# Two decode layers on one core: eight cache tiles of one position kept on chip between the two passes

## The chip, the cores and the metric

The kernel runs on one core of one Trainium2 chip. The metric is the device time of one execution in microseconds (us); less is better. Engines are named as in the profile: PE (TensorE matmul), PEld (its weight loads), DVE (VectorE), ACT (ScalarE), POOL (GpSimd), SP (SyncE, which here only issues transfers).

## The reference

Two rows of 448 numbers (a batch of two, one token each) go through attention, a gated feed-forward layer (FFN), the same attention again and the same FFN again. The two attention layers read the **same** key and value caches and weights:

```python
B, Sq, D = 2, 1, 448;  H, Sk, Dh = 16, 4096, 256;  F = 1792      # all float32
def _A_ref(x, k_cache, v_cache, wq, wo):        # caches: [2, 16, 4096, 256]
    q = (x @ wq).reshape(B, Sq, H, Dh).transpose(0, 2, 1, 3)
    p = softmax(einsum("bhqd,bhkd->bhqk", q, k_cache) * Dh ** -0.5)
    return einsum("bhqk,bhkd->bhqd", p, v_cache).transpose(...).reshape(B, Sq, H * Dh) @ wo
def _B_ref(x, W_gate, W_up, W_down):
    gate = x @ W_gate
    return (gate * (gate > 0) * (x @ W_up)) @ W_down
x = A_x
for _ in range(2):
    x = x + _A_ref(layernorm(x), A_k_cache, A_v_cache, A_wq, A_wo)
    x = x + _B_ref(layernorm(x), B_W_gate, B_W_up, B_W_down)
```

Each (head, batch) pair has 4096 keys and 4096 values of 256 numbers, 4 MiB each, so that one pass over both caches reads 256 MiB.

## The kernel before

**Units.** The work of a pass is cut into 32 units, one per (head, batch). A unit's keys lie as 32 tiles of 128 partitions x 256 numbers (128 KiB a tile, 1 KiB per partition), its values likewise. The first pass (`first`) goes through the units in order; the second (`second`) takes the last four first, in reverse order, and then units 0 to 27, so that tiles left over from the end of the first pass are used at once (`keep`, `KEPT`). Position 12 of the first pass is therefore position 16 of the second.

**The arena.** All cache tiles and weights land in one SBUF tile, `arena`: three blocks of eight slots (`BLOCKS`, `PAIR`), each slot eight cache tiles wide (`UNIT`, 1 MiB), and three single slots for weights (`SINGLES`). In the middle of each pass one transfer fills a whole block: four slots of the values of the unit before and four slots of the keys of this unit, 128 rows of 16384 numbers, 8 MiB. A list of loads (`pending`) is written in program order; `pump` issues its head on SP's queue as soon as enough slots are free, and `release`, called when a slot has been read for the last time, runs `pump`. SP waits for the releasing instruction, and later loads wait behind it. A block is free only when its four key slots and its four value slots are.

**One unit, at position u.** `score_block` multiplies all 32 key tiles in place by the query (`tensor_mul`, one DVE instruction over 8192 numbers a partition, L378) and sums each tile (`reduce_sum`, L386). `softmax_max` and `softmax_exp` take the maximum over all keys through POOL (L429) and the exponential on ACT (L434, L437); POOL also adds the sums up (L443). `weigh` then multiplies the probabilities of unit u-1 with its values on PE: 16 matmuls, which the trace shows as 32, into one of two PSUM banks (`po`, L462). `out_copy` on ACT (L475), `out_add` on DVE (L478), `out_turn` on PE (L488) and `project` (L511) bring the result into the output. Order within a turn of the loop is the order of the code: score u, `out_add` and `out_turn` of u-2, softmax of u, then `weigh` and `out_copy` of u-1. Each engine works through its own list in that order.

**Between the passes** `ffn` runs the FFN: `proj` (L576) makes gate and up, `ph` and `ph_tail` turn the hidden row, `block` (L669) multiplies with the third weight, and beside that the query of the second pass's first unit is put together (`ask`, L722 to L748). For the layer norm in it a row of column sums of the query weights is needed: `cols` in PSUM, copied by ACT, scaled, to `turn_cols`, which lies in the last 256 numbers of a weight slot (L637).

**PSUM** has eight banks: one for `pq`, two for `po`, two for `small`, one for `acc`, and two for `pf`, which the queries of each pass's first units and the FFN use in turn.

Of the kernel before, what the change touches and what calls it, by code (L numbers as in the profile page):

```python
# [26 lines left out]
KEPT = 20  # L27
ALONE = 25

SUMS = 96  # L30
# [40 lines left out]
def two_layers(  # L71
# [17 lines left out]
    ps_a = ctx.enter_context(tc.tile_pool(name="ps_a", bufs=1, space=PSUM))  # L89
    ps_f = ctx.enter_context(tc.tile_pool(name="ps_f", bufs=2, space=PSUM))  # L90
# [9 lines left out]
    blocks = set()  # L100

    def source(key, n):
# [12 lines left out]
    def pump():  # L115
        while pending:
            (kind, name, c), n = pending[0]
            last = at_of.get((kind, name, c - 1)) if kind in "kv" else None
            at = units.take(n, kind, last)
            if at is None:  # L120
                return
            pending.pop(0)
            src = source((kind, name, c), n)
            dst = arena[:, at * UNIT : at * UNIT + src.shape[1]]
            parts = [0, src.shape[1]]
            if not pending:
                parts[1:1] = [src.shape[1] - CLOSE * TAIL]
            elif len(pending) == 1:
                parts[1:1] = [8 * P]
            for i, j in zip(parts, parts[1:]):  # L130
                nc.sync.dma_start(dst[:, i:j], src[:, i:j])
            for k in range(n):
                key = (kind, name, c + k)
                if n == PAIR:
                    key = ("k", name, k - NC) if k >= NC else ("v", behind[name], k)
                at_of[key] = at + k
            if n >= NC:
                blocks.add((kind, name))

    def get(*key):  # L140
        at = at_of[key]
        return arena[:, at * UNIT : (at + 1) * UNIT]

# [88 lines left out]

    po_all = ps_o.tile([P, 2, 2 * DH], F32, name="po")
    nc.vector.memset(po_all, 0.0)

# [59 lines left out]
    def attention(order, after, q_first=None, begun=None):  # L295
# [60 lines left out]
        def first_query():  # L356


            if q_first is None:
                total = squares()  # L360
                query_of(0, ps_f.tile([P, B, DH], F32, name="pf"))
            else:
                q_of[0] = q_first
                total = begun()
            deviation(total)
            query_of(1, ps_f.tile([P, B, DH], F32, name="pf"))
            unread = work.tile([P, 1], F32, name="sums")
            nc.scalar.activation(unread, eps_t, AF.Exp)

        def score_block(u, c):  # L370


            at = at_of["k", order[u], 0] * UNIT
            kt = arena[:, at : at + NC * UNIT].rearrange("p (t n) -> p t n", t=NT)
            if c == 0:
                s_of[u] = work.tile([P, NT], F32, name="scores")
            if c == 0:
                nc.vector.tensor_mul(kt, kt, q_of[u][:, None, :].to_broadcast([P, NT, DH]))  # L378
            shared = 0 if (WHOLE_SECOND if ahead else WHOLE_FIRST)[0] <= u < ALONE else CT
            if c == 0:  # L380
                for t in range(shared):
                    nc.scalar.activation(  # L382
                        kt[:, t, :], kt[:, t, :], AF.Copy, accum_out=s_of[u][:, t : t + 1]
                    )
            if c == NC - 1:
                nc.vector.reduce_sum(s_of[u][:, shared:], kt[:, shared:, :], axis=AX.X)  # L386
# [65 lines left out]
        def weigh(u, c):  # L452
# [5 lines left out]
            if c == 0:  # L458
                po_of[u] = po_all[:, u % 2]
            for t in range(CT // 2):  # L460
# [99 lines left out]
    def ffn(last):  # L560
# [8 lines left out]

        def proj(parts):  # L570

            p = ps_f.tile([P, D], F32, name="pf")
            for n, (part, c, done) in enumerate(parts):
# [40 lines left out]

        pg = proj([(0, 0, True), (1, 1, True), (2, 2, True), (3, 3, False)])
        add_rows(SUMS, lead, stop=last)
# [6 lines left out]
        inverse()  # L623
        scaled = work.tile([P, B], F32, name="scaled")
        nc.vector.tensor_mul(scaled, sel, rstd)
        nc.vector.tensor_mul(scaled, scaled, rstd)
        if not last:
            nscaled = work.tile([P, B], F32, name="nscaled")
# [5 lines left out]
        pu = proj([(3, 4, True), (4, 0, True), (5, 1, True), (6, 2, True)])  # L634
        if not last:
            turn_cols = w_q[:, FULL * DH + P + 2 * D :]
            nc.scalar.activation(turn_cols, cols, AF.Copy, scale=nscaled[:, b : b + 1])  # L637
        nc.vector.tensor_mul(hid, pu, hid)
# [3 lines left out]

        ph = ps_f.tile([P, FULL, P], F32, name="pf")
        ph_tail = ps_q.tile([P, P], F32, name="pq")
        for m in range(FULL):
# [29 lines left out]
        if last:  # L675


            square = work.tile([P, B], F32, name="square")
# [6 lines left out]
            y_end = ps_f.tile([P, TAIL], F32, name="pf")[SUMS : SUMS + B]  # L685
            nc.tensor.matmul(y_end, unit, y_end_row, start=True, stop=False)
            pds = [po_all[:, 0, :D], ps_f.tile([P, D], F32, name="pf")] * 2

# [26 lines left out]

        q = ps_f.tile([P, DH], F32, name="pf")

# [11 lines left out]

        pd = po_all[:, 0, :D]  # L730
        sums = work.tile([P, FULL + 1], F32, name="sums4")
        total = work.tile([P, 1], F32, name="sums")
        for c in range(FULL + 1):
# [3 lines left out]
            if c > 0:  # L737
                ask(c - 1)
            if c == FULL:
                nc.vector.reduce_sum(total, sums, axis=AX.X)  # L740
            pt = ps_s.tile([P, B], F32, name="small")
# [93 lines left out]
```

## Time and profile before

| | |
|---|---|
| median of 3 runs | 1320.66 us (1320.5 to 1320.78) |
| the profiled execution: its own time / its span from first to last instruction | 1320.27 us / 1318.5 us |
| read from HBM | 562.56 MB |
| busy: PE / DVE / ACT / POOL | 553.7 / 1081.6 / 195.6 / 269.0 us |
| share of the span in which the 16 transfer engines are busy with SP's queue | 99.5% |

In the rows quoted below, a row of the timeline or the chain begins with its start and its length in us; `x2` is a count; what stands in brackets is the idle time of that engine just before, and what ended it. A row of a group of instructions ends in total busy time and the mean in ns of one. `arena<-in_vk_dram` is a load of cache tiles.

### The profile page before, as it was taken

The numbers are of one execution on the slowest core, as the hardware profiler recorded it, in microseconds if no ns is written. First come the engines' busy times: TensorE is split into PE (matmuls) and PEld (weight loads), VectorE is DVE, ScalarE is ACT, GpSimd is POOL, SyncE is SP. The second block draws the span as 40 slices with busy tenths as digits, with TensorE's granted clock in tenths as the row PEclk, the third lists the DMA queues.
The fourth block names the chain that finished last, engine by engine and source line by source line (L and its number), as shares of the span: only waits on it lengthen the run. The fifth ranks groups of instructions, "written<-read, shape, count | busy, mean of one in ns | idle before, by whom it ended". The sixth has DMA issues, their size and how long they took to land.

```text
span 1318.5 us, 9085 instructions
## 1 busy us (share of the span) xinstructions
PE 553.7 (42%) x3276; PEld 190.6 (14%) x3276; DVE 1081.6 (82%) x780; ACT 195.6 (15%) x776; POOL 269.0 (20%) x192
## 2 busy tenths in 40 slices
PE   2243342433434324345585444242433424434348
PEld 2011010110111101112141111110111101101113
DVE  4989888898888988888729987798888988877892
ACT  2100000000000000212026513000000000012241
POOL 0002003322133220321001153030123331230210
PEclk9675666656667667666697777666767667666679
DMA  9999999999999999999999999999999999999998
GB/s 408 435 430 429 432 428 437 432 436 434 417 445 435 430 430 426 445 418 430 421 405 416 431 430 435 438 432 430 432 431 436 433 428 436 429 432 425 427 425 334
DMA packets 22665, 563.16 MB, mean 427 GB/s; under 512 B 2520, under 2 KB 2652, under 8 KB 9564
## 3 DMA queue, kind: packets, MB, share of 16 engines
q1 hardware_dynamic: 22612, 562.57, 99.5%
q8 instruction: 26, 0.43, 0.1%
q14 instruction: 19, 0.16, 0.0%
q10 hardware_dynamic: 8, 0.00, 0.0%
HBM read 562.56 MB, written 0.00 MB: 427 GB/s over the span
## 4 chain that ended last, share of the span: by engine, by line
DMA 55%; DVE 32%; PE 7%; POOL 2%; issue 2%; ACT 1%; DVEq 0%; SPq 0%; POOLq 0%; ACTq 0%
DMA arena<-in_vk_dram 54%; DVE arena L378 12%; DVE scores L386 11%; DVE arena L409 3%; DVE down L418 2%; PE po L462 2%; POOL top L429 2%; DVE arena L418 2%; DMA arena<-in_w_out_dram 1%; DVE row L478 1%; PE small L488 1%; PE acc L511 1%; DVE scores L415 1%; ACT arena L411 1%; PE pf L576 1%
## 5 line engine op out<-in xcount | busy, mean ns | idle before, releaser
L378 DVE TENSOR_TENSOR arena<-arena 128x8192 f32<-128x8192 f32 x51 | 443.3, 8692 | 111.0 <-DMA arena<-in_vk_dram 110.9
L386 DVE TENSOR_REDUCE scores<-arena 128x32 f32<-128x8192 f32 (+1 forms) x53 | 431.8, 8148 | 0.0
L488 PE MATMUL small<-ones,row 128*128 128x1 f32 x256 | 62.0, 346 | 686.3 <-DVE row L478 686.3
L462 PE MATMUL po<-arena,probs 128*2 128x512 f32 x2048 | 303.1, 734 | 10.3 <-DMA arena<-in_vk_dram 6.6
L429 POOL PARTITION_ALL_REDUCE top<-mx x64 | 64.6, 1009 | 645.8 <-DVE mx L427 645.8
L443 POOL PARTITION_ALL_REDUCE total<-rs x64 | 176.1, 2752 | 61.3 <-ACT probs L437 60.3
L488 PEld LDWEIGHTS small<-ones,row 128*128 128x128 f32 x256 | 56.5, 308 | 748.9 <-DVE row L478 748.9
L434 ACT ACTIVATE nm<-top,nsr 128x1 f32<-128x1 f32 x64 | 18.8, 294 | 612.4 <-POOL top L429 612.4
L354 POOL PARTITION_BROADCAST arena<-arena x58 | 27.6, 545 | 300.6 <-ACT arena L350 300.6
L462 PEld LDWEIGHTS po<-arena,probs 128*2 128x2 f32 x2048 | 54.8, 96 | 198.3 <-issue 191.2
L338 PE MATMUL pq<-arena,xs 128*33 128x256 f32 x174 | 70.6, 571 | 14.1 <-DMA arena<-in_w_head_dram 14.1
L511 PE MATMUL acc<-arena,oT 128*2 128x448 f32 x128 | 50.9, 894 | 32.1 <-DVE oT L501 32.1
L350 ACT ACTIVATE arena<-pq 33x256 f32<-33x256 f32 x29 | 10.9, 377 | 321.7 <-PE pq L342 321.7
L382 ACT ACTIVATE arena<-arena 128x256 f32<-128x256 f32 x104 | 41.7, 402 | 86.2 <-DVE arena L378 86.2
L478 DVE SCALAR_TENSOR_TENSOR row<-po,lead,row 128x256 f32<-128x256 f32 x64 | 30.7, 479 | 25.8 <-ACT row L475 25.4
L411 ACT ACTIVATE arena<-arena 128x256 f32<-128x256 f32 x117 | 47.1, 404 | 20.4 <-DVE arena L409 20.1
L409 DVE TENSOR_TENSOR arena<-arena 128x1024 f32<-128x1024 f32 (+1 forms) x24 | 42.0, 1748 | 0.0
L338 PEld LDWEIGHTS pq<-arena,xs 128*33 128x33 f32 x174 | 25.3, 162 | 81.3 <-issue 66.7
L475 ACT ACTIVATE row<-po,lead 128x256 f32<-128x256 f32 x64 | 29.1, 455 | 21.2 <-PE po L462 21.2
L418 DVE SCALAR_TENSOR_TENSOR down<-arena,pq 128x256 f32<-128x256 f32 x64 | 26.9, 420 | 5.4 <-DMA arena<-in_vk_dram 3.4
L501 DVE TENSOR_TENSOR oT<-small,ri 128x4 f32<-128x4 f32 x32 | 5.1, 161 | 29.0 <-PE small L488 29.0
L437 ACT ACTIVATE probs<-scores,nm,sr 128x32 f32<-128x32 f32 x64 | 26.4, 413 | 2.1
(145 smaller groups left out, 359.0 us busy)
## 6 DMA issues: line engine op xcount, KB each, us to landing
arena<-in_vk_dram SPq DMA_DIRECT2D x16, 4096.0 KB, 40.0
arena<-in_w_head_dram SPq DMA_DIRECT2D x31, 896.0 KB, 30.9
arena<-in_vk_dram SPq DMA_DIRECT2D x27, 1024.0 KB, 14.9
arena<-in_vk_dram SPq DMA_DIRECT2D x12, 2048.0 KB, 38.5
arena<-in_w_in_dram SPq DMA_DIRECT2D x14, 896.0 KB, 26.2
arena<-in_w_out_dram SPq DMA_DIRECT2D x5, 896.0 KB, 8.9
arena<-in_vk_dram SPq DMA_DIRECT2D x47, 43.4
arena<-in_w_out_dram SPq DMA_DIRECT2D x1, 512.0 KB, 17.3
```

Source lines behind the costliest of these rows:

```text
L338: nc.tensor.matmul(q, xs[:, c, :], w[:, c * DH : (c + 1) * DH], start=(c == 0), stop=False)
L378: nc.vector.tensor_mul(kt, kt, q_of[u][:, None, :].to_broadcast([P, NT, DH]))
L386: nc.vector.reduce_sum(s_of[u][:, shared:], kt[:, shared:, :], axis=AX.X)
L409: nc.vector.tensor_mul(some, some, q_of[u][:, None, :].to_broadcast([P, whole, DH]))
L411: nc.scalar.activation(kt[:, t, :], kt[:, t, :], AF.Copy, accum_out=found[:, t : t + 1])
L418: nc.vector.scalar_tensor_tensor(junk if kept else kt[:, t, :], kt[:, t, :], 1.0, q_of[u], op0=ALU.mult, op1=ALU.mult, accum_out=found[:, ...
L429: nc.gpsimd.partition_all_reduce(mx_of[u], mx, P, RED.max)
L443: nc.gpsimd.partition_all_reduce(total[:, b : b + 1], rs, P, RED.add)
L462: nc.tensor.matmul(po_of[u][32 * t : 32 * t + 2, :], p_of[u][:, n : n + 2], vt[:, 2 * t * DH : (2 * t + 2) * DH], start=(c == 0), stop=(c ...
L478: nc.vector.scalar_tensor_tensor(row[:, :DH], po_of.pop(u)[:, DH:], lead[:, 1:2], row[:, :DH], op0=ALU.mult, op1=ALU.add,)
L488: nc.tensor.matmul(pT_of[u - u % 2][:, c, b : b + 1], row[:, c * P : (c + 1) * P], ones, start=True, stop=True,)
L511: nc.tensor.matmul(acc[at : at + B], oT_of[h][:, c, :], wo[:, c * D : (c + 1) * D], start=(n < 3), stop=(n >= n_u - 3),)
```

## The change

Eight tiles that the first pass loads at position 12 stay on the chip and are not read again in the second pass.

- **Keys.** The last four key tiles of the unit at position 12 are copied by ACT, before they are overwritten, into two PSUM banks (`spare`, two tiles each). In the second pass DVE multiplies and sums them there: three multiplications and three sums in place of one each. In the first pass the multiplication is split in two, since its second part must wait for the copies.
- **Values.** The first four value tiles of the unit at position 11, which come with the same block, are copied by ACT into 1024 numbers per partition at the end of `arena` (`extra`). PE reads these four tiles from the copy, in both passes.
- **Traffic.** The block's transfer in the second pass is 128 rows of 14336 numbers, not 16384: 1 MiB less. All else is loaded as before, in the same order and into the same slots.
- **Room.** The single slots are 1792 instead of 2048 numbers wide (all that the weights fill), several small tiles share buffers (`scaled` is now named `nm`, `nscaled` `top`, `square` `mx`, `sums4` `rs`), and 768 bytes fewer are set aside for descriptors of transfers issued by POOL, of which there are none. What used `pf` uses the two `po` banks in turn, now two tiles, or in the last FFN the two `spare` banks.
- **Column sums.** `cols` stays in its bank (`pq`) until the FFN's end, where DVE scales it into `row`; ACT's copy is gone. `ph_tail` goes to a `small` bank, since `pq` is taken.

```diff
+SPARED = 12
+KEYS = 4
+VALUES = 4
...
-    arena = consts.tile([P, (BLOCKS * PAIR + SINGLES) * UNIT], F32, name="arena")
+    ps_f = ctx.enter_context(tc.tile_pool(name="ps_f", bufs=1, space=PSUM))
+    arena = consts.tile([P, BLOCKS * PAIR * UNIT + SINGLES * F + VALUES * DH], F32, name="arena")
+    extra = arena[:, -VALUES * DH :]
...
     def source(key, n):
+            if name in spared and n == PAIR:
+                return vk[at, :, VALUES * DH : PAIR * UNIT - KEYS * DH]
...
     def pump():
-            dst = arena[:, at * UNIT : at * UNIT + src.shape[1]]
+            start = place(at) + VALUES * DH * (name in spared and n == PAIR)
+            dst = arena[:, start : start + src.shape[1]]
...
+    po = [ps_o.tile([P, 2 * DH], F32, name=f"po{i}") for i in range(2)]
+    spare = [ps_f.tile([P, 2 * DH], F32, name=f"spare{i}") for i in range(2)]
...
         def score_block(u, c):
+            there = [(kt, 0)]
+            if order[u] == first[SPARED]:
+                most = NT - KEYS
+                held = [bank.rearrange("p (t n) -> p t n", t=2) for bank in spare]
+                there = [(kt[:, :most], 0)]
+                there += [(part, most + 2 * i) for i, part in enumerate(held)]
+                if not ahead:
+                    if c == 0:
+                        for part, t in there[1:]:
+                            nc.scalar.activation(part, kt[:, t : t + 2, :], AF.Copy)
+                        spared.add(order[u])
+                    there[1:] = [(kt[:, most:], most)]
             if c == 0:
-                nc.vector.tensor_mul(kt, kt, q_of[u][:, None, :].to_broadcast([P, NT, DH]))
+                for part, t in there:
+                    n = part.shape[1]
+                    nc.vector.tensor_mul(
+                        part, part, q_of[u][:, None, :].to_broadcast([P, n, DH])
+                    )
...
             if c == NC - 1:
-                nc.vector.reduce_sum(s_of[u][:, shared:], kt[:, shared:, :], axis=AX.X)
+                if shared or not ahead:
+                    there = [(kt[:, shared:, :], shared)]
+                for part, t in there:
+                    found = s_of[u][:, t : t + part.shape[1]]
+                    nc.vector.reduce_sum(found, part, axis=AX.X)
...
         def weigh(u, c):
+            held = c == 0 and order[u] == first[SPARED - 1]
+            if held and not ahead:
+                nc.scalar.activation(extra, vt[:, : VALUES * DH], AF.Copy)
             for t in range(CT // 2):
...
-                    vt[:, 2 * t * DH : (2 * t + 2) * DH],
+                    (extra if held and 2 * t < VALUES else vt)[:, 2 * t * DH : (2 * t + 2) * DH],
...
     def ffn(last):
+        banks = spare if last else po
...
-            turn_cols = w_q[:, FULL * DH + P + 2 * D :]
-            nc.scalar.activation(turn_cols, cols, AF.Copy, scale=nscaled[:, b : b + 1])
...
-        ph_tail = ps_q.tile([P, P], F32, name="pq")
+        ph = banks[0][:, : FULL * P].rearrange("p (m r) -> p m r", m=FULL)
+        ph_tail = ps_s.tile([P, P], F32, name="small")
...
-        pd = po_all[:, 0, :D]
+        pd = po[1][:, :D]
         for c in range(FULL + 1):
             at = block(pd, c, range(14))
...
             if c == FULL:
+                turn_cols = row[:, :DH]
+                nc.vector.tensor_scalar_mul(turn_cols, cols, nscaled[:, b : b + 1])
                 nc.vector.reduce_sum(total, sums, axis=AX.X)
```

Where instructions move: in the fences below, the names after `L` are lines of the one kernel and of the other; `po_108` and `po_109` are the two `po` banks, `spare_112` and `spare_113` the two new ones.

ACT's list around position 12 of the first pass, before: the exponential of one unit is followed directly by `out_copy` (L475) of the unit before it.

```order
L434 ACTIVATE nm<-top,nsr 128x1
L437 ACTIVATE probs,rs<-scores,nm,sr 128x32
L475 ACTIVATE row<-po,lead 128x256
L350 ACTIVATE arena<-pq 33x256
L434 ACTIVATE nm<-top,nsr 128x1
```

The same place after, from the copies of the keys (L400) on:

```order
L400 ACTIVATE spare_112<-arena 128x512
L400 ACTIVATE spare_113<-arena 128x512
L468 ACTIVATE nm<-top,nsr 128x1
L471 ACTIVATE probs,rs<-scores,nm,sr 128x32
L496 ACTIVATE arena<-arena 128x1024
L512 ACTIVATE row<-po_109,lead 128x256
```

The copy of the value tiles (L496) stands behind the exponential of unit 12, and PE's `weigh` of unit 11 reads what it writes.

DVE's list at the end of the FFN between the passes, from the product of gate and up on, before:

```order
L638 TENSOR_TENSOR row<-pf,row 128x448
L652 COPY row<-pf 128x384
L747 TENSOR_TENSOR xs<-xs,small 128x32 x3
L740 TENSOR_REDUCE sums<-sums_1780 128x1
L747 TENSOR_TENSOR xs<-xs,small 64x32 x2
```

and after:

```order
L674 TENSOR_TENSOR row<-po_109,row 128x448
L688 COPY row<-po_108 128x384
L785 TENSOR_TENSOR xs<-xs,small 128x32 x3
L777 TENSOR_SCALAR row<-pq,top 128x256
L778 TENSOR_REDUCE sums<-rs 128x1
L785 TENSOR_TENSOR xs<-xs,small 64x32 x2
```

The scaling of the column sums (L777) now stands on DVE ahead of the sum (L778) that PE's last part of the query waits for; it writes over part of `row`, which PE's `block` matmuls read.

DVE's list at the spared unit in the second pass (position 16), after; before, it was one multiplication and one sum like its neighbours:

```order
L406 TENSOR_TENSOR arena<-arena 128x7168
L406 TENSOR_TENSOR spare_112<-spare_112,arena 128x512
L406 TENSOR_TENSOR spare_113<-spare_113,arena 128x512
L515 SCALAR_TENSOR_TENSOR row<-po_108,lead,row 128x256
L484 RECIPROCAL ri<-total 128x2
L420 TENSOR_REDUCE scores<-arena 128x28
L420 TENSOR_REDUCE scores<-spare_112 128x2
L420 TENSOR_REDUCE scores<-spare_113 128x2
```

Four instructions have come in, two on each side of the row that `out_add` makes.

More of the change, by code (lines that the diff above doesn't have):

```diff
@@ L100, in two_layers @@
     blocks = set()
+    spared = set()
     def source(key, n):
@@ L138, in pump, with place @@
                 blocks.add((kind, name))
+    def place(at):
+        packed = max(0, at - BLOCKS * PAIR)
+        return at * UNIT - packed * (UNIT - F)
     def get(*key):
         at = at_of[key]
-        return arena[:, at * UNIT : (at + 1) * UNIT]
+        return arena[:, place(at) : place(at + 1)]
     def release(*key):
@@ L231, in two_layers @@
     rstd = consts.tile([P, B], F32, name="rstd")
-    po_all = ps_o.tile([P, 2, 2 * DH], F32, name="po")
-    nc.vector.memset(po_all, 0.0)
+    po = [ps_o.tile([P, 2 * DH], F32, name=f"po{i}") for i in range(2)]
+    for bank in po:
+        nc.vector.memset(bank, 0.0)
+    spare = [ps_f.tile([P, 2 * DH], F32, name=f"spare{i}") for i in range(2)]
     acc = ps_a.tile([P, D], F32, name="acc")
@@ L568, in ffn, with proj @@
             w_q = get("h", h, 0)
-        def proj(parts):
-            p = ps_f.tile([P, D], F32, name="pf")
+        banks = spare if last else po
+        def proj(p, parts):
+            p = p[:, :D]
             for n, (part, c, done) in enumerate(parts):
@@ L611, in between @@
                     )
-        pg = proj([(0, 0, True), (1, 1, True), (2, 2, True), (3, 3, False)])
+        pg = proj(banks[0], [(0, 0, True), (1, 1, True), (2, 2, True), (3, 3, False)])
         add_rows(SUMS, lead, stop=last)
@@ L623, in ffn @@
         inverse()
-        scaled = work.tile([P, B], F32, name="scaled")
+        scaled = work.tile([P, B], F32, name="nm")
         nc.vector.tensor_mul(scaled, sel, rstd)
@@ L627, in ffn @@
         if not last:
-            nscaled = work.tile([P, B], F32, name="nscaled")
+            nscaled = work.tile([P, B], F32, name="top")
             nc.vector.tensor_scalar_mul(nscaled, scaled, -1.0 / D)
@@ L633, in ffn @@
             cols = ps_q.tile([P, DH], F32, name="pq")
-        pu = proj([(3, 4, True), (4, 0, True), (5, 1, True), (6, 2, True)])
-        if not last:
-            turn_cols = w_q[:, FULL * DH + P + 2 * D :]
-            nc.scalar.activation(turn_cols, cols, AF.Copy, scale=nscaled[:, b : b + 1])
+        pu = proj(banks[1], [(3, 4, True), (4, 0, True), (5, 1, True), (6, 2, True)])
         nc.vector.tensor_mul(hid, pu, hid)
@@ L712, in ffn @@
             return
-        q = ps_f.tile([P, DH], F32, name="pf")
+        q = po[0][:, :DH]
         def ask(c):
@@ L728, in ask @@
                 )
-        pd = po_all[:, 0, :D]
-        sums = work.tile([P, FULL + 1], F32, name="sums4")
+        pd = po[1][:, :D]
+        sums = work.tile([P, FULL + 1], F32, name="rs")
         total = work.tile([P, 1], F32, name="sums")
@@ L828 @@
     from concourse.bass_utils import run_bass_kernel_spmd as _run
-    nc = _bacc.Bacc("TRN2", target_bir_lowering=False, num_devices=1, dynamic_dma_scratch_size=1024)
+    nc = _bacc.Bacc("TRN2", target_bir_lowering=False, num_devices=1, dynamic_dma_scratch_size=256)
     arrays = _arrays(_np, **inputs)
```

14 lines of the change are left out of this document (6 added, 8 removed).

## The prediction

> **What bounds the kernel now.** I read the page's slices first, to see whether any engine or the transfers are busy throughout.
>
> ```profile
> DVE  4989888898888988888729987798888988877892
> DMA  9999999999999999999999999999999999999998
> q1 hardware_dynamic: 22612, 562.57, 99.5%
> arena<-in_vk_dram SPq DMA_DIRECT2D x47, 43.4
> ```
>
> DVE, the busiest engine, has gaps in most slices. The transfers have none before the last slice. The last row is the 47 whole-block loads: 43.4 us from issue to landing. Next the stages, cut at the FFN between the passes and at the end; the last two columns are the share of time in which the transfer engines are busy and their GB/s.
>
> ```profile
> 2.00:660.00 658.00, 260.54 (x1399) 87.97 (x1403) 557.36 (x367) 63.01 (x228) 130.35 (x93) 0.66 1.00 431
> 668.00:672.00 4.00, 3.90 (x37) 1.23 (x36) 0.94 (x6) 0.02 (x1) 0.00 (x0) 1.00 0.79 297
> 672.00:1300.00 628.00, 266.57 (x1599) 91.80 (x1597) 517.33 (x381) 127.32 (x536) 138.27 (x94) 0.69 1.00 430
> 860.00:1160.00 300.00, 112.77 (x638) 36.37 (x638) 263.11 (x76) 20.02 (x67) 69.57 (x44) 0.67 1.00 432
> 1300.00:1310.00 10.00, 9.78 (x79) 3.31 (x77) 2.75 (x12) 0.70 (x2) 0.00 (x0) 1.00 1.01 414
> 1310.00:1318.50 8.50, 5.42 (x128) 3.63 (x126) 1.84 (x8) 1.49 (x6) 0.00 (x0) 1.00 0.26 99
> ```
>
> The transfers run full from 2 to 668 us and from 672 to 1310 us. The one hole, 668 to 672 us, is 0.21 x 4 = 0.84 us of idle; after 1310 us only the last weights and the tail are left. So time is bytes over rate, and the next question is how far ahead of DVE the queue runs. These are DVE's multiplications at positions 15 to 17 of the second pass (the spared unit is 16), and SP's longest wait:
>
> ```profile
> 954.02 8.69 DVE L378 TENSOR_TENSOR arena<-arena 128x8192 f32<-128x8192 f32 x1 [1.31 <-DMA arena<-in_vk_dram]
> 975.64 8.69 DVE L378 TENSOR_TENSOR arena<-arena 128x8192 f32<-128x8192 f32 x1 [2.45 <-DMA arena<-in_vk_dram]
> 994.93 8.69 DVE L378 TENSOR_TENSOR arena<-arena 128x8192 f32<-128x8192 f32 x1 [1.33 <-DMA arena<-in_vk_dram]
> SPq L131 <- DVE scores L386: 697.4, 52, 34.4
> ```
>
> DVE waits for data at each unit, 1.3 to 2.45 us. SP waits for DVE to free a block, but that does not hurt: of the 43.4 us of a block load, its own 8.39 MB at 432 GB/s are 19.4 us, so 24.0 us pass between the issue and its first bytes, nearly all of it other loads. That is the cover of every step below in this stretch.
>
> **Part 1, the bytes.** Eight tiles are 8 x 131072 = 1.049 MB fewer. In the stage that holds position 16 (860 to 1160 us) the rate is 432 GB/s: 2.43 us less. Nearest rows for other rates: 414 GB/s (narrow weight rows, 1300 to 1310 us) gives 2.53 us, so 2.4 to 2.55 us. I take 2.43, because the shortened rows stay long. By the Trainium skill's "HBM Reference", section "Specifications (TRN2)", a core's share of HBM is about 358 GB/s, by which the same bytes would be worth an estimated 2.93 us; the trace disagrees, with 432 GB/s on this core alone.
>
> **Does the gain reach the end?** The chain of waits, in order of time:
>
> ```profile
> 1177.20 43.65 DMA arena<-in_vk_dram
> 1220.97 8.69 DVE arena L378
> ...
> 1300.25 14.69 DMA arena<-in_w_out_dram
> ```
>
> The last block starts DVE at 1220.97 us, and from there to 1300.25 us the chain holds no transfer: DVE and then PE set the releases of the last loads. A block that lands 2.43 us sooner starts that stretch 2.43 us sooner, since DVE is idle ahead of each of the units between, and the last loads are still queued (14.69 us from issue to landing of one piece). So all of it moves together.
>
> **Part 2, position 12 of the first pass.** What stands there now; the multiplications are those of units 12 and 13:
>
> ```profile
> 262.60 8.69 DVE L378 TENSOR_TENSOR arena<-arena 128x8192 f32<-128x8192 f32 x1 [2.48 <-DMA arena<-in_vk_dram]
> 272.68 6.52 PE L462 MATMUL po<-arena,probs 128*2 128x512 f32 x32
> 280.41 0.33 SPq L131 DMA_DIRECT2D arena<-in_vk_dram  x1
> 280.65 0.35 POOL L429 PARTITION_ALL_REDUCE top<-mx  x1 [18.67 <-DVE mx L427]
> 281.68 0.19 ACT L437 ACTIVATION_READ_ACCUMULATOR probs<-scores,nm,sr 128x1 f32 x1
> 281.91 8.69 DVE L378 TENSOR_TENSOR arena<-arena 128x8192 f32<-128x8192 f32 x1 [1.36 <-DMA arena<-in_vk_dram]
> 281.95 8.89 POOL L443 PARTITION_ALL_REDUCE total<-rs  x1 [0.96 <-ACT probs L437]
> 290.52 0.48 DVE L478 SCALAR_TENSOR_TENSOR row<-po,lead,row 128x256 f32<-128x256 f32 x1
> 294.08 0.33 SPq L131 DMA_DIRECT2D arena<-in_w_head_dram  x1
> L475 ACT ACTIVATE row<-po,lead 128x256 f32<-128x256 f32 x64 | 29.1, 455 | 21.2 <-PE po L462 21.2
> L382 ACT ACTIVATE arena<-arena 128x256 f32<-128x256 f32 x104 | 41.7, 402 | 86.2 <-DVE arena L378 86.2
> L263 ACT ACTIVATE row<-row 2x448 f32<-2x448 f32 x1 | 0.6, 575 | 0.0
> ```
>
> ACT takes 402 ns for 256 numbers and 575 for 448, 0.9 ns each: about 0.63 us for 512 and 1.09 us for 1024. No row shows ACT writing PSUM; between 0.4 us (the 256-wide row) and twice 0.63, I take 0.63, as the row nearest in width is 575. The two key copies end near 263.9 us, long before DVE has done its first 28 tiles (7.6 of the 8.69 us, to 270.2). They cost DVE one instruction more, some 0.1 us, inside its 1.36 us of idle.
>
> The value copy costs more in order than in time. It stands behind unit 12's exponential, which ends at 281.87, so ends near 283.0. `weigh` of unit 11, now at 272.68, waits for it: 6.52 us of matmuls, done at 289.5. Three things stand behind. `out_copy` on ACT then ends near 290.0 (0.45 us), and DVE wants it at 290.52: just in time, and if not, DVE's idle of some 2 us a unit takes it. `out_turn` on PE follows DVE as before. And the load that SP issued at 280.41 goes out near 289.5, as its block now holds unit 11's values until then: 9.1 us later, out of 24.0 us of cover. SP's next load, a head's weights, was issued 13.67 us after, so nothing queues up behind. Cost nothing; without that cover, 9.1 us.
>
> **Part 3, position 16 of the second pass.** The sum that unit 16 has now, and DVE's nearest row with a wide PSUM input:
>
> ```profile
> 984.72 8.66 DVE L386 TENSOR_REDUCE scores<-arena 128x32 f32<-128x8192 f32 x1
> L638 DVE TENSOR_TENSOR row<-pf,row 128x448 f32<-128x448 f32 x2 | 1.2, 624 | 7.9 <-PE pf L576 7.9
> ```
>
> 624 ns for 448 against 8.69 us for 8192 (1.06 ns each): 512 numbers take 0.55 us by the long row and 0.71 by the short one. Two multiplications and two sums of 512 instead of 1024 more in each long one: 4 x 0.71 - 2 x 1.09 = 0.7 us more; if writing PSUM doubled the multiplications, 2.1 us. No row shows that write; I take 0.7, as the row nearest in size says. DVE's 2.45 us of idle ahead of unit 16 let it start with its data, 2.43 us sooner; unit 17's data come sooner by as much, and the 1.33 us of idle ahead of that unit hold the 0.7. At 2.1 DVE would be 0.8 us late there, gone by the next unit's idle, and SP's releases with it, under the 24.0 us. Cost nothing. PE reads four value tiles at another address, which costs nothing either.
>
> **Part 4, the FFN between the passes**, where the queue is thinnest. The end of the query's chain, and the six 1 MiB loads issued from 690 to 705 us:
>
> ```profile
> 686.02 0.64 PE L669 MATMUL po<-arena,row 128*32 128x64 f32 x28
> 686.13 0.19 DVE L747 TENSOR_TENSOR xs<-xs,small 128x32 f32<-128x32 f32 x1 [1.66 <-PE small L744]
> 687.05 0.16 DVE L740 TENSOR_REDUCE sums<-sums 128x1 f32<-128x4 f32 x1 [0.74 <-ACT down L736]
> 687.43 0.70 PE L748 MATMUL pf<-arena,sums 128*128 128x256 f32 x2
> 688.62 0.42 DVE L418 SCALAR_TENSOR_TENSOR arena<-arena,pf 128x256 f32<-128x256 f32 x1 [0.66 <-PE pf L725]
> arena<-in_vk_dram SPq DMA_DIRECT2D x6, 1024.0 KB, 8.3
> SPq L131 <- PE pf L576: 5.9, 3, 5.2
> ```
>
> The scaling of `cols` on DVE writes over `row`, so it waits for the last `block` matmul (686.66) and takes about 0.45 us (256 numbers from PSUM; L478 above takes 0.48), to 687.15; the sum then ends at 687.3 instead of 687.21, ahead of L748 at 687.43. Cost 0 to 0.45 us on this chain. A load here lands 8.3 us after issue, 2.5 us of it its own bytes, so 5.8 us, less its start-up, lie ahead of it: 0.45 us is covered. The hole at 668 to 672 us comes earlier: SP waits for the first PE matmuls of `proj` (the last row, from 664 to 672 us), which no edit delays. It stays. The new PSUM banks add only waits for reads long done; I cost the renamed buffers at nothing too.
>
> **The sum.** 1320.27 (this execution; 1318.5 of it the span) - 2.43 = 1317.84. The median of the runs lies 0.39 above this execution, so 1320.66 - 2.43 = **1318.2 us**. 0.2%, about what a measurement of this kernel can tell from no change, is 2.64 us: below 1318.02 counts as faster. The forecast is 0.184%, just inside.
>
> **The rivals.**
> - *More than the bytes* (0.24): the bytes are worth 2.55 us and the hole of 0.84 us in part closes, as the releases there shift. Against it: no edit is ahead of the hole. Up to 2.55 + 0.84 = 3.39 us: 1317.3. By 0.25 us above forecast it counts as faster. The skill's 358 GB/s would land here too, at 1320.66 - 2.93 = 1317.7 us; I give that 0.02 of the 0.24.
> - *Part of the gain is lost* (0.10): the thin queue after the FFN runs dry for a while, or the stretch from 1220.97 us turns out bound by DVE and PE alone, and then the last loads come no sooner. For it: no transfer in that part of the chain. Against: it starts with one. 1318.5 to 1320.7.
> - *Slower, by the late release at position 12* (0.06): the block load that leaves at 280.41 now hangs on ACT, behind POOL's maximum. It decides at 24.0 us of delay, when the queue runs dry; 9.1 is the sum above. If PE's `weigh` also had to sit out POOL's 8.89 us row and one more unit (20.45 us, half the 40.91 us between the multiplications of positions 15 and 17), 38.4 us late, 14.4 us dry: 1320.66 - 2.43 + 14.4 = 1332.7. With one unit alone, 29.6 us late and 5.6 dry: 1323.8. For it: the one new wait that a load hangs on. Against: the maximum takes 0.35 us there.
> - That the change does not do what it says is ruled out by the load itself, 14336 numbers wide instead of 16384.
>
> **How the numbers follow.** Forecast 0.60, rivals 0.24, 0.10, 0.06. The forecast's own spread (0.14 us of the runs, 2.4 to 2.55 us of the bytes, 0.45 us of Part 4) is 1317.9 to 1318.7, with a small part below 1318.02. Faster: 0.24 and 0.04 of the forecast, 0.28. Same: 0.56 and 0.10, 0.66. Slower: 0.06. The range, leaving out the slow rival and the ends of the two others: 1317.4 to 1319.3.
>
> **What would show it.** Right: HBM read 1.05 MB less; transfers still 0.99 to 1.01 busy in all stages but 668 to 672 us, where the hole stays near 0.84 us; `weigh` of unit 11 near 283 us, and a block load issued near 289.5 that still lands before DVE wants it, three units after 262.60; unit 17 of the second pass starting about 2.4 us sooner than 994.93. Wrong: a stage with a share below 0.97 after 283 us or after 690 us, a DVE wait above 3 us at positions 13 to 16 of the first pass, or a tail after the last load other than now.

## The result, and the profile after

| | before | after |
|---|---|---|
| median, same chip | 1320.81 us (1320.5 to 1321.43, 15 runs) | 1318.33 us (1317.98 to 1318.87, 15 runs) |
| the profiled execution / its span | 1320.27 / 1318.5 us | 1318.33 / 1316.6 us |
| read from HBM | 562.56 MB | 561.52 MB |

After over before is 0.9982 (95% interval 0.9975 to 0.9988): 2.48 us less, against a forecast of 2.43.

The page of the kernel after: slices of DVE and of the transfers, the loads' queue, HBM, and two of the issues (size where it is even, and us from issue to landing). The row with 7168.0 KB is the block load that has become narrower.

```profile
DVE  4989888898888988788829987698898988877892
DMA  9999999999999999999999999999999999999998
q1 hardware_dynamic: 22612, 561.53, 99.5%
...
HBM read 561.52 MB, written 0.00 MB: 427 GB/s over the span
...
arena<-in_vk_dram SPq DMA_DIRECT2D x1, 7168.0 KB, 41.0
...
arena<-in_vk_dram SPq DMA_DIRECT2D x46, 43.2
```

The stages of the kernel after, cut as in the prediction (the last three columns: PE's granted clock, the transfers' busy share, GB/s):

```profile
2.00:660.00 658.00, 256.65 (x1393) 88.89 (x1394) 557.59 (x369) 65.27 (x231) 137.81 (x93) 0.68 1.00 431
668.00:672.00 4.00, 3.91 (x43) 1.95 (x44) 1.55 (x10) 0.74 (x1) 0.00 (x0) 1.00 0.69 244
672.00:1300.00 628.00, 273.86 (x1623) 92.98 (x1622) 519.16 (x391) 126.89 (x535) 146.25 (x94) 0.68 1.00 429
860.00:1160.00 300.00, 114.85 (x638) 36.82 (x638) 265.82 (x80) 20.05 (x67) 78.28 (x44) 0.66 1.00 433
```

The picture is that of before: transfers full in both passes at the same rate, and one hole at 668 to 672 us. The hole is larger here, 0.31 x 4 = 1.24 us against 0.84; the experiments come back to that.

### The profile page after: what moved, and what is told of

It reads as the page before. It is cut to its first block, busy times and chain, and to the rows that moved or that the text cites. A ratio compares the mean times of both kernels' runs of the same rounds, so it can differ in the third digit from the quotient of the medians.

```text
span 1316.6 us, 9091 instructions
## 1 busy us (share of the span) xinstructions
PE 555.1 (42%) x3276; PEld 192.1 (15%) x3276; DVE 1082.8 (82%) x787; ACT 197.4 (15%) x778; POOL 284.4 (22%) x192
## 3 DMA queue, kind: packets, MB, share of 16 engines
HBM read 561.52 MB, written 0.00 MB: 427 GB/s over the span
## 4 chain that ended last, share of the span: by engine, by line
DMA 56%; DVE 30%; PE 7%; POOL 3%; issue 2%; ACT 1%; SPq 0%; DVEq 0%; POOLq 0%; ACTq 0%
DMA arena<-in_vk_dram 53%; DVE scores L420 11%; DVE arena L406 11%; POOL top L463 3%; DVE down L452 2%; PE po L499 2%; DMA arena<-in_w_in_dram 2%; DVE arena L443 2%; DVE arena L452 2%; DMA arena<-in_w_out_dram 1%; DVE row L515 1%; PE small L525 1%; PE acc L548 1%; PE pq L352 1%; ACT arena L445 1%
## 5 line engine op out<-in xcount | busy, mean ns | idle before, releaser
L406 DVE TENSOR_TENSOR arena<-arena 128x8192 f32<-128x8192 f32 (+2 forms) x52 | 442.3, 8507 | 105.3 <-DMA arena<-in_vk_dram 104.6
L420 DVE TENSOR_REDUCE scores<-arena 128x32 f32<-128x8192 f32 (+2 forms) x53 | 430.8, 8128 | 0.0
L463 POOL PARTITION_ALL_REDUCE top<-mx x64 | 80.4, 1256 | 626.0 <-DVE mx L461 626.0
L352 PE MATMUL pq<-arena,xs 128*33 128x256 f32 x174 | 74.7, 597 | 13.1 <-DMA arena<-in_w_head_dram 13.1
L445 ACT ACTIVATE arena<-arena 128x256 f32<-128x256 f32 x117 | 47.1, 404 | 20.4 <-DVE arena L443 20.1
## 6 DMA issues: line engine op xcount, KB each, us to landing
arena<-in_vk_dram SPq DMA_DIRECT2D x1, 7168.0 KB, 41.0
```

The source lines that it names most:

```text
L352: nc.tensor.matmul(q, xs[:, c, :], w[:, c * DH : (c + 1) * DH], start=(c == 0), stop=False)
L406: nc.vector.tensor_mul(part, part, q_of[u][:, None, :].to_broadcast([P, n, DH]))
L420: nc.vector.reduce_sum(found, part, axis=AX.X)
L445: nc.scalar.activation(kt[:, t, :], kt[:, t, :], AF.Copy, accum_out=found[:, t : t + 1])
L463: nc.gpsimd.partition_all_reduce(mx_of[u], mx, P, RED.max)
```

## The experiments

Two theories stood at the start. **Bytes**: the kernel is bound by its transfers, the gain is the 1 MiB not read, and all edits around it are covered by the queue. **Sum of edits**: the 2.48 us are a larger gain, less what the copies, the late release or the FFN edits cost. The rival to the cover itself is that a late release costs more, or less, than its delay beyond the queue.

### All edits but the bytes, and the bytes alone

`e1_all_but_bytes` is the kernel after, loading the whole block again in pass 2, so that the spared tiles are read and not used:

```diff
-            if name in spared and n == PAIR:
-                return vk[at, :, VALUES * DH : PAIR * UNIT - KEYS * DH]
...
-            start = place(at) + VALUES * DH * (name in spared and n == PAIR)
+            start = place(at)
```

> The changed kernel in all its edits (copies, split multiplications, PSUM operands, column sums in PSUM, renamed buffers), but the block at position 16 of the second pass is loaded whole again, 16384 numbers a row. Theory 'bytes over rate': the other edits cost and earn nothing, so the time of the kernel before comes back, 1320.8 us within 0.3 us (ratio 0.9998 to 1.0002). Rival 'the other edits earn part of it' (one ACT copy less between the passes, other PSUM banks): 1318.4 to 1320.3 us. Rival 'the other edits cost, and the bytes earn more than 2.43 us' (by a core's share of 358 GB/s 2.93 us): 1321.2 us or more.

Measured: 1320.36 us (1319.88 to 1320.82, 11 runs) beside 1320.85 of the kernel before; ratio 0.9997 [0.9989, 1.0006]. That is 0.14 us below the expected range and not as low as either rival put it; `e6_no_tiles_spared` comes back to it.

`e2_bytes_alone` is the kernel before with the narrower load in pass 2 and nothing else; the eight tiles there are computed from what an earlier load left in the slots.

```diff
...
+            if name == first[12] and n == PAIR and name in seen:
+                return vk[at, :, 4 * DH : PAIR * UNIT - 4 * DH]
...
-            dst = arena[:, at * UNIT : at * UNIT + src.shape[1]]
+            start = at * UNIT + 4 * DH * (name == first[12] and n == PAIR and name in seen)
+            dst = arena[:, start : start + src.shape[1]]
+            if n == PAIR:
+                seen.add(name)
```

> The kernel before with one edit: the block at position 16 of the second pass is loaded 14336 numbers wide, and nothing is copied, so that eight tiles of that position are computed from old contents of the arena. Theory 'bytes over rate': 2.43 us less than before, 1318.4 us within 0.3 us (ratio 0.9980 to 0.9983). Rival 'the other edits earn part': less than 2.0 us gained here. Rival 'other edits cost': more than 2.8 us gained here.

Measured: 1318.24 us (1317.8 to 1319.1, 11 runs); ratio 0.9981 [0.9972, 0.999]. The bytes alone give what the whole change gives, and all the rest together gives nothing that can be told from no change.

### Four times the bytes

`e3_bytes_x4` is `e2_bytes_alone` with 16 tiles in place of 4 left out at each end of the block: 4 MiB less.

```diff
-                return vk[at, :, 4 * DH : PAIR * UNIT - 4 * DH]
+                return vk[at, :, 16 * DH : PAIR * UNIT - 16 * DH]
...
-            start = at * UNIT + 4 * DH * (name == first[12] and n == PAIR and name in seen)
+            start = at * UNIT + 16 * DH * (name == first[12] and n == PAIR and name in seen)
```

> The same with four times the bytes: 16 value tiles and 16 key tiles of that position are not loaded (8192 numbers a row, 4 MiB), and are computed from old contents of the arena. Theory 'bytes over rate': 4.194 MB at 432 GB/s, 9.71 us less: 1311.1 us, since DVE, though late by more than its idle of 2.45 us at that unit, has some 1.3 to 2.45 us of idle at each of the 13 units after it. Rival 'DVE bounds the end': the last stretch, where the chain holds no transfer, does not come sooner by more than DVE can make up; 1313 to 1317 us. Rival '358 GB/s': 11.7 us less, 1309.1 us.

Measured: 1310.88 us (1310.76 to 1310.98, 5 runs); ratio 0.9926 [0.9914, 0.9939]. That is 9.97 us, 2.49 us for each MiB (by the interval 2.0 to 2.8). The gain is linear in the bytes and reaches the end whole, so no engine takes over as the bound. The Trainium skill's "SBUF — State Buffer", section "The DMA setup-cost knee (why "@ 1 MiB" ≠ asymptote)", gives 436 GB/s as the rate that transfers tend to as they grow; by it a MiB would be an estimated 2.41 us, and the runs agree with that to within their interval. The 2.93 us that the prediction worked out from the Trainium skill's "HBM Reference", section "Specifications (TRN2)", lies above that interval. That section of the Trainium skill gives 358 GB/s as a core's share while both cores of a domain stream, and about 425 GB/s for a core that streams alone. The second is this kernel's case, and the trace is close to it with 432 GB/s; the prediction had taken the first.

### A later release at position 12

The release that the change made late was made later still. `e4a_release_19us_late` frees the value slots of the unit at position 11 only after `weigh` of the unit at position 12:

```diff
...
-            if ("v", order[u], c) not in after:
+            if not ahead and u == SPARED - 1:
+                late.append(("v", order[u], c))
+            elif ("v", order[u], c) not in after:
                 release("v", order[u], c)
+            if not ahead and u == SPARED - 1 + 1 and c == NC - 1:
+                for key in late:
+                    release(*key)
```

> The changed kernel, but the four value slots of unit 11 in the first pass are given free only after PE's weigh of unit 12, near 300 us, some 19.6 us after the 280.4 of the kernel before and 11.4 after the 288.6 of the changed kernel. Theory of cover (24.0 us of other loads ahead of a block load, less its start-up): still hidden, 1318.3 us within 0.4 us. Rival 'a release that comes late costs its time': up to 11 us more, 1329 us.

Measured: 1319.16 us (1318.39 to 1319.49, 11 runs); ratio 0.9988 [0.9979, 0.9996]. The load in SP's timeline of this kernel:

```profile
300.77 0.33 SPq L140 DMA_DIRECT2D arena<-in_vk_dram  x1
```

Its stretch from 296 to 312 us:

```profile
296.00:312.00 16.00, 4.15 (x35) 0.91 (x33) 13.09 (x3) 1.54 (x5) 1.69 (x4) 0.71 0.89 369
```

The same stretch of the kernel after:

```profile
296.00:312.00 16.00, 4.04 (x33) 0.68 (x32) 13.09 (x3) 1.54 (x5) 1.69 (x4) 0.71 0.97 422
```

The load leaves 20.4 us later than before the change (300.77 less 280.41), and the queue has just begun to run dry: 0.89 busy against 0.97. DVE starts unit 15 1.58 us later than in the kernel after, where it starts at 322.98 us:

```profile
324.56 8.69 DVE L407 TENSOR_TENSOR arena<-arena 128x8192 f32<-128x8192 f32 x1 [2.80 <-DMA arena<-in_vk_dram]
```

At the last block 0.75 us of that is left (1219.82 us against 1219.07). The time lies outside the expected 1318.3 within 0.4 us, and far below the rival's 1329. The 0.83 us between the medians of this kernel and the kernel after lie inside the overlap of their intervals: the load is no longer fully hidden, but the price at the end is not settled by this run.

`e4b_release_39us_late` moves the release one `weigh` further (`SPARED - 1 + 2`).

> The kernel after, but the value slots of the unit at position 11 are freed only after `weigh` of the unit at position 13, so that the block load that went out at 288.56 us after the change and at 280.41 us before goes out near 319 us. Theory (what hides the late release is the queue ahead of that load, which ran dry with 20.4 us of delay): 38.7 us of delay less 20 to 21 us of cover leave 17 to 18 us in which the transfers stand still: 1335 to 1337 us. Rival 1 (the whole 24.0 us are cover): 14.7 us, 1333. Rival 2 (DVE's idle, a good 2 us a unit, takes back part of a late load): below 1330 us.

Measured: 1319.64 us (1318.57 to 1321.17, 9 runs); ratio 0.9986 [0.9968, 1.0004]. That is far below the theory and the first rival; it lies where the second rival put it, but not by its mechanism, as SP's timeline of this kernel says:

```profile
300.51 0.33 SPq L140 DMA_DIRECT2D arena<-in_vk_dram  x1
321.32 0.80 SPq L140 DMA_DIRECT2D arena<-in_vk_dram  x2
```

The slots were held, the load was not. `pump` takes whichever block is free, and at 300.5 us that was the next one, whose values `weigh` of unit 12 had just read. So the first load was no later than in the run before, and only the second waited, with the first still ahead of it in the queue. DVE starts unit 15 1.80 us later than in the kernel after and unit 16 1.72 us (346.34 against 344.62), so the second load's wait cost nothing of its own. The run does not bear on how far the cover reaches; its expectation had left the allocator out.

`e4c_both_blocks_held` holds the value slots of both units, so that no block can be free:

```diff
...
-            if not ahead and u == SPARED - 1:
+            if not ahead and u in (SPARED - 1, SPARED):
```

> The kernel after, but the value slots of the units at positions 11 and 12 are both freed only after `weigh` of the unit at position 13. Holding those of position 11 alone did not delay the next load by more than 20 us, since the next block that came free took it (it went out at 300.5 us); now no block is free before about 321 us, so that three block loads go out together there, the first of them 40.9 us later than before the change. Theory (20 to 20.5 us of delay are covered, and every us beyond is lost at the end): 1318.3 plus 20 to 21 us, 1338 to 1340 us, and the transfers stand still from about 302 to 322 us. Rival 1 (all 24.0 us are cover): 16.9 us, 1335. Rival 2 (a stop in the transfers is partly made good, by DVE's idle time or by a faster rate after it): below 1334 us.

Measured: 1338.84 us (1338.17 to 1338.89, 3 runs); ratio 1.0135 [1.0115, 1.0155]. The load and unit 15 in the timelines of SP and DVE of this kernel:

```profile
321.92 0.33 SPq L140 DMA_DIRECT2D arena<-in_vk_dram  x1
343.81 8.69 DVE L407 TENSOR_TENSOR arena<-arena 128x8192 f32<-128x8192 f32 x1 [21.75 <-DMA arena<-in_vk_dram]
```

Two stretches of it:

```profile
300.00:302.00 2.00, 0.24 (x4) 0.00 (x0) 1.31 (x2) 0.09 (x1) 0.35 (x1) 1.00 0.61 262
302.00:322.00 20.00, 7.08 (x36) 1.90 (x36) 17.86 (x5) 1.06 (x4) 0.38 (x1) 0.66 0.00 1
```

The load leaves at 321.92, 41.5 us later than before the change. The transfers stand still from about 302 to 322 us, DVE waits 21.75 us for unit 15, and the end is 1338.84 - 1318.33 = 20.5 us later. So next to nothing of a stop is made good, and the cover is 41.5 - 20.5 = 21.0 us. The traces say nearly the same: from its issue to DVE's start on unit 15 the load took 322.82 - 280.41 = 42.4 us in the kernel before, and 343.81 - 321.92 = 21.9 us here, with nothing ahead of it, which leaves 20.5 us for the queue. The 21.9 us are 2.5 us more than the 19.4 us of its own bytes; the prediction had counted that start-up as cover. Both rivals (1335 and below 1334) fall. Nor is the edge sharp: with 20.4 us of delay, in `e4a_release_19us_late`, unit 15 already started 1.58 us late.

### The rest of the change by itself

`e6_no_tiles_spared` keeps the room, the column sums in PSUM and the banks used in turn, and spares no tile (two lines):

```diff
-            if order[u] == first[SPARED]:
+            if order[u] is None:
...
-            held = c == 0 and order[u] == first[SPARED - 1]
+            held = c == 0 and order[u] is None
```

> The kernel after without its spared tiles: every block load 16384 numbers wide, no copies, no work on the spare banks; what is left of the change is the room, the column sums that stay in PSUM, and the banks used in turn. Forecast's reading (these edits cost and earn nothing): the time of the kernel before, 1320.85 us in this chip's runs. Rival (they earn some 0.5 us, as the run with a whole load and all other edits hinted with 1320.36): 1320.35 us.

Measured: 1320.55 us (1320.3 to 1322.1, 11 runs) beside 1320.59; ratio 1.0000 [0.9991, 1.0009]. No cost or gain of these edits can be told from nothing. The 0.49 us by which `e1_all_but_bytes` lay lower did not come back; this run leaves the copies and the split work out too, so of those it says nothing.

### The hole between the passes

By the first profiles, the time of an execution seemed to go with its hole at 668 to 672 us: with the bytes added back, 1320.23 at 0.72 us (`e1_all_but_bytes`) up to 1321.35 at 1.40 (`e2_bytes_alone`). Two runs tried that. `e7_before_again` is the kernel before once more; in `e5_one_slot_less_kept` a slot more is free between the passes, so that SP needn't wait there:

```diff
-KEPT = 20
+KEPT = 19
```

> The kernel before, unchanged, for a second profile. Theory (the time differs from run to run with the size of the hole between the passes, which hangs on PE and not on an edit): the hole at 668 to 672 us lies between 0.7 and 1.4 us, and this execution's time less the hole is 1319.4 to 1320.0 us, as in the first profile (1320.27 - 0.84 = 1319.43). Rival (the hole belongs to the kernel): 0.84 us again, whatever the time.

> The kernel after with KEPT 19 in place of 20: one slot of 1 MiB fewer stays from pass 1 to pass 2 and is loaded again, and stands free between the passes, so that the sixth load of FFN weights needn't wait for PE there. Theory (the hole between the passes delays every byte behind it): plus 2.43 us for the bytes, less the hole of 0.8 to 1.4 us: 1319.4 to 1320.0 us, transfers busy in 668 to 672 us, and times that spread less from run to run. Rival (the hole costs nothing at the end, or only moves): 1320.8 us.

Measured: `e7_before_again` 1320.67 us (1320.27 to 1320.92, 11 runs; ratio 1.0000 [0.9991, 1.0008]), its profiled execution 1320.87. `e5_one_slot_less_kept` 1320.75 us (1320.46 to 1321.24, 11 runs; ratio 0.9999 [0.999, 1.0008]). The hole in `e7_before_again`:

```profile
668.00:672.00 4.00, 3.91 (x38) 1.25 (x36) 0.94 (x6) 0.04 (x1) 0.00 (x0) 1.00 0.79 297
```

The same stretch in `e5_one_slot_less_kept`:

```profile
668.00:672.00 4.00, 3.91 (x40) 1.39 (x40) 1.08 (x7) 0.21 (x1) 0.00 (x0) 1.00 0.99 394
```

In its timelines, SP's sixth load of FFN weights (the first of the two in the row), and the block of pass 2 that I follow from here:

```profile
657.30 12.66 SPq L139 DMA_DIRECT2D arena<-in_w_in_dram  x2
833.00 8.69 DVE L406 TENSOR_TENSOR arena<-arena 128x8192 f32<-128x8192 f32 x1 [13.09 <-DMA arena<-in_vk_dram]
```

The same two of the kernel after:

```profile
670.17 1.08 SPq L139 DMA_DIRECT2D arena<-in_w_in_dram  x2
830.81 8.69 DVE L406 TENSOR_TENSOR arena<-arena 128x8192 f32<-128x8192 f32 x1 [11.54 <-DMA arena<-in_vk_dram]
```

The theory falls in both. In the kernel before the hole was 0.84 us again and that execution 0.60 us longer, so the hole does not carry the spread from run to run (1320.87 - 0.84 = 1320.03, 0.03 above what was expected). In the other, the hole is gone (0.99 busy), the runs spread no less (0.78 us against 0.65), and the time is 2.42 us above the kernel after (2.64 when each is set against the kernel before on its own chip): the byte price of the reloaded slot, and nothing back for the filled hole. The rival held. The interval of the ratio alone, 1319.3 to 1321.6 us, would leave room for the theory; the table below does not. (Its seventh load of FFN weights still waits, to 657.30 + 12.66 - 0.33 = 669.6 us, with the sixth queued.) Its block at 833.00 starts 2.19 us after that of the kernel after, whose sixth load went out 13 us later. Adding up the packets in the two traces, 206.3 MB have yet to land when DVE starts on that block, against 206.7 in the kernel after, though the loads that remain are the same: 0.4 MB, 1.0 us, went to loads behind the one that DVE waited for. Part of the hole may thus be time in which what is needed next was in flight anyway; that is not shown, and which of the 16 transfer engines are late there was not taken apart.

What does move with the hole is its far edge. Over the profiled executions without a held release, DVE's start on unit 12 of the first pass, the issue of the sixth load, and the start of that block on DVE:

| kernel | unit 12 starts | sixth load issued | block starts |
|---|---|---|---|
| `e1_all_but_bytes` | 262.54 | 669.41 | 830.31 |
| before | 262.60 | 669.46 | 830.35 |
| `e7_before_again` | 262.63 | 669.48 | 831.00 |
| `e6_no_tiles_spared` | 262.76 | 669.62 | 830.50 |
| `e3_bytes_x4` | 262.74 | 669.67 | 830.60 |
| after | 262.85 | 670.17 | 830.81 |
| `e2_bytes_alone` | 263.42 | 670.35 | 831.28 |
| `e5_one_slot_less_kept` | 262.70 | 657.30 | 833.00 (830.57 without its 2.43 us) |

A later issue brings a later block in all but the second profile of the kernel before; an issue 12 us sooner brings no sooner block. The issue is not set by the change: `e2_bytes_alone` differs from before in one load, some 260 us later, and yet has 670.35 against 669.46.

The first column shows that most of this lateness is older than the hole. The issue follows unit 12 by 406.85 to 406.93 us in six of the seven executions in which SP waits there (407.32 in the kernel after). The block follows unit 12 by 567.74 to 567.96 us in six of them, with holes from 0.72 to 1.40 us; in `e7_before_again` it is 568.37, and there the transfers moved 373 GB/s from 672 to 680 us, against 417 in the first profile of before. With the hole closed it is 830.57 - 262.70 = 567.87 us, the same again. So the hole grows when an execution is late already, and costs nothing that can be seen. What makes executions differ ahead of unit 12 stays open.

## Why the prediction was right

**The bytes.** 2.43 us were forecast at 432 GB/s; 2.48 us were measured for the change, 2.61 for the bytes alone, 2.49 per MiB for four. The rate in the stage of position 16 was 433 GB/s. That 2.43 and 2.48 agree so closely is in part luck: the interval of the ratio leaves anything from 1.6 to 3.3 us, and the two profiled executions differ by 1.94. What bears the price out is the run with 4 MiB less. The prediction took 0.2% for about the least that can be told from no change; with 15 runs of each kernel the interval of this 0.18% leaves out 1.

**Does the gain reach the end?** The end of the chain of waits of the kernel after:

```profile
1175.10 43.84 DMA arena<-in_vk_dram
1219.07 8.69 DVE arena L406
1235.65 39.09 DMA arena<-in_vk_dram
1274.80 24.29 DMA arena<-in_w_in_dram
1299.17 13.85 DMA arena<-in_w_out_dram
```

The last block starts DVE 1.90 us sooner than in before (1220.97), the last weights are in flight 1.08 us sooner (1300.25), and the span is 1.9 us shorter in these two executions. From 1235.65 us this chain runs through transfers, where that of before ran through DVE and PE until 1300.25: the two are nearly level there. The rival *part of the gain is lost* needed DVE and PE alone to set that stretch; in `e3_bytes_x4` the end came 9.97 us sooner.

**Position 12 of the first pass.** The timeline of the kernel after:

```profile
262.75 1.12 ACT L400 ACTIVATE spare<-arena 128x512 f32<-128x512 f32 x2 [0.61 <-DMA arena<-in_vk_dram]
262.85 8.76 DVE L406 TENSOR_TENSOR arena<-arena 128x7168 f32<-128x7168 f32 x2 [2.47 <-DMA arena<-in_vk_dram]
282.10 1.04 ACT L496 ACTIVATE arena<-arena 128x1024 f32<-128x1024 f32 x1
283.19 5.25 PE L499 MATMUL po<-arena,probs 128*2 128x512 f32 x32 [10.12 <-ACT arena L496]
288.52 0.47 ACT L512 ACTIVATE row<-po,lead 128x256 f32<-128x256 f32 x1 [5.38 <-PE po L499]
288.56 0.33 SPq L139 DMA_DIRECT2D arena<-in_vk_dram  x1
290.70 0.48 DVE L515 SCALAR_TENSOR_TENSOR row<-po,lead,row 128x256 f32<-128x256 f32 x1
322.98 8.69 DVE L406 TENSOR_TENSOR arena<-arena 128x8192 f32<-128x8192 f32 x1 [1.29 <-DMA arena<-in_vk_dram]
```

Unit 15 in the timeline of the kernel before:

```profile
322.82 8.69 DVE L378 TENSOR_TENSOR arena<-arena 128x8192 f32<-128x8192 f32 x1 [1.31 <-DMA arena<-in_vk_dram]
```

Step by step: ACT wrote 512 numbers to PSUM in 0.56 us (0.63 forecast) and copied 1024 in 1.04 (1.09); `weigh` of unit 11 waited 10.12 us for that copy and began at 283.19 (near 283); it took 5.25 us, not 6.52, so the load left at 288.56 (289.5), 8.15 us late; `out_copy` at 288.52 was ready for DVE at 290.70. Unit 15 started at 322.98 against 322.82 in before, with 1.29 us of idle: hidden, as forecast. The rival *slower, by the late release* had its mechanism right and its deciding point too far out: not 24.0 us of delay but 20.5 to 21.0, as the load's own start-up comes off the cover. Its 14.4 us for 38.4 us of delay would have been 17.4 to 17.9.

**Position 16 of the second pass.** DVE in the timeline of the kernel after:

```profile
973.65 7.62 DVE L406 TENSOR_TENSOR arena<-arena 128x7168 f32<-128x7168 f32 x1
981.19 1.29 DVE L406 TENSOR_TENSOR spare<-spare,arena 128x512 f32<-128x512 f32 x2
983.22 7.60 DVE L420 TENSOR_REDUCE scores<-arena 128x28 f32<-128x7168 f32 x1
990.74 1.28 DVE L420 TENSOR_REDUCE scores<-spare 128x2 f32<-128x512 f32 x2
992.95 8.69 DVE L406 TENSOR_TENSOR arena<-arena 128x8192 f32<-128x8192 f32 x1 [0.71 <-DMA arena<-in_vk_dram]
```

An operation on 512 numbers in PSUM took about 0.65 us, a multiplication that writes there like a sum that only reads (0.71 forecast; the doubling that was the upper bound is not there). From the start of unit 16 to the end of its sums are 18.37 us against 17.74 before: 0.63 us more, 0.7 forecast. They come out of DVE's idle ahead of unit 17, 0.71 us against 1.33. Unit 17 starts at 992.95, 1.98 us sooner than before; position 15 started 0.41 us later (954.43 against 954.02), so the spared load brought 2.39.

**The FFN between the passes.** The query's chain in the timeline of the kernel after:

```profile
686.60 0.64 PE L705 MATMUL po<-arena,row 128*32 128x64 f32 x28
687.20 0.48 DVE L777 TENSOR_SCALAR row<-pq,top 128x256 f32<-128x256 f32 x1 [0.30 <-PE po L705]
687.64 0.16 DVE L778 TENSOR_REDUCE sums<-rs 128x1 f32<-128x4 f32 x1
688.01 0.70 PE L786 MATMUL po<-row,sums 128*128 128x256 f32 x2
```

From the last `block` matmuls to the query's last part are 688.01 - 686.60 = 1.41 us, and 687.43 - 686.02 = 1.41 before. The scaling cost nothing, the lower end of 0 to 0.45.

**The hole** did stay, but "near 0.84 us" was one execution's number: it was 0.72 to 1.40 us over the seven profiles of the table in which SP waits there. The rival *more than the bytes* rested in part on closing it; with the hole closed nothing was gained, so that rival had less for it than the prediction gave.

## What to carry to other kernels

Where the transfers are busy from end to end, price a change by its bytes at the rate of its own stage, and ask of every other edit only whether it makes a load leave later than the queue ahead of it lasts; the time from issue to landing, less the load's own bytes and 3 to 3.5 us here, is about that cover. A late release cost nothing well inside it (8.15 us), showed on DVE at its edge (20.4 us), and cost its full length beyond it (20.5 of 41.5 us); but which load it delays is up to the allocator, so follow the slot and not the name. An idle stretch of the transfer engines is not a gain in waiting until a run has filled it; and where it seems to go with the time from execution to execution, see whether the execution was late before it.

## What was not expected of the hardware

A stop of some 20 us in the transfers came back at the end as 20.5 us, though DVE idles 1.3 to 2.5 us a unit: that idle is only time spent waiting for the same transfers. And a hole of 0.84 us in the transfers' busy share, filled, was worth nothing that 11 runs could show.
